# Sorted attention and a gated feed-forward on one core: five value blocks sorted from the loaded tile, and the first stage's calls listed anew

## The chip, the core and the metric

The kernel runs on one core of a Trainium2 chip. The core has TensorE for matrix products (with a separate row for its weight loads), VectorE, ScalarE and GpSimd (POOL) for the rest, and SyncE, which here issues transfers only. All engines take their instructions in order. The metric is the device time of one execution in microseconds; the kernel before takes 231.41 us, the median of three runs (231.49, 230.86, 231.41).

## The reference

```
for _ in range(5):                                   # P: sort_net, 8 x 8 per head
    P = exp(P - max(P, -1)); P = P / (sum(P, -1) + 1e-9); P = P / (sum(P, -2) + 1e-9)
k_sorted = einsum('bhij,bhjcd->bhicd', P, k_blocks)  # 8 blocks of 96 keys
v_sorted = einsum('bhij,bhjcd->bhicd', P, v_blocks)
scores = (q_block @ k_sorted_block.T) / 8            # each block attends to its own block
attn   = softmax(scores);  x = attn @ v_sorted_block
h = x @ w_in;  out = (h * cos(h)) @ w_out
```

There are 4 batches of 8 heads, 768 positions and 64 columns, so x is 3072 x 512; w_in is 512 x 2048 and w_out 2048 x 512. Output is 3072 x 512 in float32.

## The kernel before

The 3072 rows are cut into eight **chunks** n of 384 rows: batch n // 2, and the first or second four blocks of 96 positions. A chunk has four units u, one block of positions each, for all eight heads. Per unit: scores (`s_ps`, later `qs`, `bt`), their maximum and difference on VectorE (`s_max`, `s_sub`, or `qk_reduce`), the exponential on ScalarE (`expo`), its transpose (by TensorE as `p_ps` and `p_ev`, or by a DMA transpose from SyncE's queue), the product with the sorted values (`av_products`), its normalisation on VectorE (`av_norm`) and a second transpose (`x_ps`, `x_ev`, or `xp`, `xe`). With the chunk's rows transposed, the feed-forward runs "up" (`up_four`, `uh`: products with w_in; `cos_four`, `uc`: the cosine on ScalarE; `gate_four`, `ug`: the product on VectorE) and "down" (`down_four`, `dn`: products with w_out; `down_out`, `dc`: the copy out and its store).

Ahead of that, the 8 x 8 matrices are normalised (`rounds`, lines 346 to 394) and spread into block matrices (`bds`, `bdv`), and keys and values are sorted by products with them: `kp` and `k_place` make the first batch's keys in three tiles t, of which half 0 serves chunk 0 and half 1 chunk 1 (`kxp` copies half 1 across partitions on POOL); `ks` and `kse` those of the second batch; `v0` and `v0e` the first batch's values in eight blocks z of eight columns. The products of a block z read their weights either straight from the loaded tile (`vv`, one column every 64 elements) or from `vperm`, a copy with the columns gathered that POOL makes (`v_permute`). The constant VN (line 202) says how many of the 64 columns are read directly: below it `v0` takes `vv` and writes two results per instruction (line 798), from it on `vperm`. VN also sets how much of the second batch's half of the value tile POOL clears (line 388), how much of `vperm` ScalarE zeroes (line 366) and how much `z_vperm` clears later (line 754).

The order is written out by hand (`manual_schedule`, line 63): lines 1028 to 1561 list the calls, and each engine and each DMA queue runs its own share of them in that order. Waits between engines come from the data and from tiles that are used again: three double tiles (`big`, tag B), two single ones (`acc`, tag C), three score tiles and so on. Loads, with a cast from float32, are issued by POOL and so stand in POOL's order; DMA transposes and stores are issued by SyncE. `p_hold` and `hold` (line 613) are one-element copies on POOL that wait for a DMA transpose, so that the loads listed after them are not issued earlier. `load_pair` loads both batches of the second pair, keys into `pair`, values into `vbuf`. `keep_warm` products (`fill=`) fill waits with products of zeros.

The change touches VN; lines 1028 to 1215, which hold chunk 0 and the attention of chunk 1; the value loads at lines 1237 to 1239 and 1317; the hold at 1316; `dn(1, 1, 2)` and `dn(1, 1, 3)` at 1307 and 1311; the evictions `xe(2, 1)` and `xe(2, 0)` at 1335 and 1339; and the eviction `be("vs", 2)` at 1409.

Of the kernel before, what the change touches and what calls it, by code (L numbers as in the profile page):

```python
# [18 lines left out]
def kernel(  # L19
# [157 lines left out]
    def v_permute(rows, lo=0, halves=True, step=VQ, hi=D):  # L177

        for z in range(lo, hi, step):
            dst = vperm[rows, :CD].rearrange("p (d c) -> p d c", d=D)[:, z:z + step]
            src = vv[rows, z:z + step, :blk]
            if halves:
                dst = dst.rearrange("p d (x t) -> p d x t", x=2)
                src = src.rearrange("p d (t x) -> p d x t", x=2)
            nc.gpsimd.tensor_copy(dst, src)  # L187
# [14 lines left out]
    VN = 32  # L202
# [833 lines left out]
    kp(0, *B)  # L1036
    k_place(0, A, 0)
    k_place(0, V, 1)
    v_permute(slice(0, 64), 56, False, 8, 64)
    kp(1, *B)  # L1040
    k_place(1, A, 0)
    k_place(1, A, 1)
    v0(0, *C)
    v0e(0, A)
    s_ps(0, 0)
    s_max(0, 0)
    s_sub(0, 0)
    s_ps(0, 1)
    v0(3, *C)
    v0(2, *B)  # L1050
    v0e(3, A)
    v0e(2, A)
    s_max(0, 1)
    s_sub(0, 1)
    expo(0, 0, True)
    v0(1, *C)
    v0e(1, A)
    v0(5, *C)
    s_ps(0, 3)
    s_ps(0, 2)  # L1060
    s_max(0, 3)
    s_max(0, 2)
    v0e(5, A)
    expo(0, 1, True)
    s_sub(0, 3)
    load_w_out(0)
    v0(4, *C)
    v0e(4, A)
    v0(6, *C, fill=1)
    v0(7, *B)  # L1070
    v0e(7, A)
    p_ps(0, 1, *C, fill=2)
    p_ev(0, 1, V)
    v0e(6, A)
    expo(0, 3, True)
    p_ps(0, 0, *B, fill=2)
    p_ev(0, 0, A)
    av_products(0, 1, fill=2)
    s_sub(0, 2)
    av_norm(0, 1, True)  # L1080
    load_w_out(1)
    av_products(0, 0)
    p_ps(0, 3, *B)
    av_norm(0, 0, True)
    load_w_out(2)
    load_w_out(3)
    kxp(2)
    kxp(0)
    expo(0, 2, True)
    p_ps(0, 2, *C)  # L1090
    x_ps(0, 1, *B)
    p_ev(0, 2, V)
    x_ps(0, 0, *C)
    kxp(1)
    p_ev(0, 3, A)
    x_ev(0, 1, A)
    av_products(0, 3)
    x_ev(0, 0, V)
    av_products(0, 2)
    up_four(0, 2, 0)  # L1100
    up_four(0, 2, 1)
    cos_four(0, 2)
    av_norm(0, 3, True)
    x_ps(0, 3, *B)
    q_products(1, 0, 0, 16, *C)
    av_norm(0, 2, True)
    z_turned(1)
    load(kbuf, 0, kin_d[1])
    x_ev(0, 3, V)
    load(vbuf, 64, vin_d[1])  # L1110
    q_products(1, 1, 0, 16, *C)
    x_ps(0, 2, *B)
    x_ev(0, 2, A)
    up_four(0, 0, 0)
    gate_four(0, 2)
    up_four(0, 0, 1)
    cos_four(0, 0)
    picks(pick_pair, (2, 3))
    up_four(0, 1, 0)
    up_four(0, 1, 1)  # L1120
    cos_four(0, 1)
    gate_four(0, 0)
    up_four(0, 3, 0)
    up_four(0, 3, 1)
    up_four(1, 0, 0)
    gate_four(0, 1)
    cos_four(0, 3)
    gate_four(0, 3)
    z_vperm()
    up_four(1, 0, 1)  # L1130
    q_place_half(1, 0, 1, A)
    q_place_half(1, 0, 0, V)
    cos_four(1, 0)
    gate_four(1, 0)
    up_four(1, 2, 0)
    up_four(1, 2, 1)
    q_place_half(1, 1, 0, A)
    z_turned(0)
    q_place_half(1, 1, 1, V)
    up_four(1, 3, 0)  # L1140
    up_four(1, 3, 1)
    up_four(1, 1, 0)
    p_pads()
    down_four(1, 0)
    cos_four(1, 2)
    gate_four(1, 2)
    load_q(2)
    last = block([pick_pair[:]], *C)
    cos_four(1, 3)
    gate_four(1, 3)  # L1150
    spread(bds[1], last)
    s_ps(1, 0)
    s_max(1, 0)
    s_ps(1, 1)
    up_four(1, 1, 1)
    cos_four(1, 1)
    s_max(1, 1)
    s_sub(1, 0)
    expo(1, 0, True)
    down_four(0, 0)  # L1160
    down_four(0, 1)
    down_four(0, 2)
    ks(5, *B)
    gate_four(1, 1)
    s_sub(1, 1)
    kse(5, A)
    s_ps(1, 3)
    down_four(0, 3)
    expo(1, 1, True)
    load_pair(pair, kin_d, 0 * CD // 2, 1 * CD // 2)  # L1170
    s_max(1, 3)
    s_sub(1, 3)
    p_ps(1, 0, *B)
    s_ps(1, 2)
    s_max(1, 2)
    s_sub(1, 2)
    load_pair(pair, kin_d, 1 * CD // 2, 2 * CD // 2)
# [3 lines left out]
    down_four(1, 1)  # L1181
    p_ps(1, 1, *B)
    v_permute(slice(64, 128), 48, True, 16, 64)
    down_out(0, A)
    p_ev(1, 0, A)
    expo(1, 3, True)
    av_products(1, 0)
    av_norm(1, 0, True)
    ks(4, *C)
    down_four(1, 2)  # L1190
    p_ev(1, 1, A)
    av_products(1, 1)
    p_ps(1, 3, *B)
    p_ev(1, 3, V)
    kse(4, A)
    av_norm(1, 1, True)
    expo(1, 2, True)
    down_four(2, 0)
    p_ps(1, 2, *B)
    p_ev(1, 2, A)  # L1200
    av_products(1, 3)
    av_norm(1, 3, True)
    down_four(1, 3)
    av_products(1, 2)
    down_out(1, A)
    x_ps(1, 1, *B)
# [3 lines left out]
    x_ps(1, 0, *B)  # L1210
    x_ps(1, 3, *B)
    av_norm(1, 2, True)
# [94 lines left out]
    dn(1, 1, 2)  # L1307
# [3 lines left out]
    dn(1, 1, 3)  # L1311
    dc(1, 1, nc.sync)
# [3 lines left out]
    p_hold(2, 2)  # L1316
# [18 lines left out]
    xe(2, 1, None, V)  # L1335
# [3 lines left out]
    xe(2, 0, None, V)  # L1339
# [67 lines left out]
    bt(('vs', 1, A), ('vs', 2, A))  # L1407
    be("vs", 1, A)
    be("vs", 2, A)
# [181 lines left out]
```

## Time and profile before

| | |
|---|---|
| median of three runs | 231.41 us |
| profiled execution, its own time | 230.85 us |
| its span | 229.1 us |
| granted TensorE clock | 1.00 |
| TensorE busy | 219.3 us, 96% |
| weight loads busy | 137.4 us, 60% |
| VectorE, ScalarE busy | 171.8 us (75%), 153.0 us (67%) |
| POOL busy | 95.2 us, 42% |
| moved by DMA | 31.21 MB |

The span runs from the first to the last instruction that the profiler recorded; the profiled execution's own time is 1.75 us longer. All times inside the kernel are counted from the span's start. A row of the timeline has the start, the duration of the group, the engine, the line, the operation, the tiles and shapes and, in brackets, how long the engine idled before and what ended the wait. Durations of successive matmuls overlap, since they are pipelined. A row of transfers ends with the time from issue to landing.

### The profile page before, as it was taken

The numbers are of one execution on the slowest core, as the hardware profiler recorded it, in microseconds if no ns is written. First come the engines' busy times: TensorE is split into PE (matmuls) and PEld (weight loads), VectorE is DVE, ScalarE is ACT, GpSimd is POOL, SyncE is SP. The second block draws the span as 40 slices with busy tenths as digits, with TensorE's granted clock in tenths as the row PEclk, the third lists the DMA queues.
The fourth block names the chain that finished last, engine by engine and source line by source line (L and its number), as shares of the span: only waits on it lengthen the run. The fifth ranks groups of instructions, "written<-read, shape, count | busy, mean of one in ns | idle before, by whom it ended". The sixth has DMA issues, their size and how long they took to land.

```text
span 229.1 us, 5513 instructions
## 1 busy us (share of the span) xinstructions
PE 219.3 (96%) x2243; PEld 137.4 (60%) x2265; DVE 171.8 (75%) x297; ACT 153.0 (67%) x206; POOL 95.2 (42%) x120
## 2 busy tenths in 40 slices
PE   8688899999999999999999999999999999999994
PEld 3387798567665566645665456655655566555554
DVE  6779859987798768868589967987699769646700
ACT  5749865966989758897688466736674667716521
POOL 7999999299960288934517001800000000000000
PEclk9999999999999999999999999999999999999999
DMA  5999999996999699857979639953934440351012
GB/s 65 237 187 207 204 205 234 198 230 172 99 120 206 172 157 132 146 126 152 165 146 129 118 70 164 201 92 73 189 119 85 89 158 0 69 147 46 0 46 94
DMA packets 67833, 31.21 MB, mean 136 GB/s; under 512 B 56416, under 2 KB 63200, under 8 KB 67552
## 3 DMA queue, kind: packets, MB, share of 16 engines
q0 software_dynamic: 24048, 13.64, 43.4%
q1 hardware_dynamic: 43472, 17.02, 33.8%
q8 instruction: 18, 0.29, 0.6%
q10 hardware_dynamic: 288, 0.20, 0.3%
q14 instruction: 7, 0.06, 0.1%
HBM read 27.27 MB, written 6.29 MB: 147 GB/s over the span
## 4 chain that ended last, share of the span: by engine, by line
PE 80%; DVE 12%; ACT 4%; issue 2%; DMA 1%; ACTq 0%; DVEq 0%
PE h L687 18%; PE o L712 16%; PE h L915 14%; PE o L1012 11%; PE av L643 3%; DVE mx L839 3%; DVE s L843 3%; PE sc L457 3%; PE h L876 2%; PE ks L424 2%; PE o L897 2%; DVE gg L888 2%; PE o L1555 2%; ACT p_buf L587 1%; PE xps L966 1%
## 5 line engine op out<-in xcount | busy, mean ns | idle before, releaser
L687 PE MATMUL h<-xT,w_in_t 128*128 128x384 bf16 x256 | 43.2, 327 | 0.0
L691 ACT ACTIVATE c<-h,half_pi 128x768 f32<-128x768 f32 x32 | 28.8, 900 | 17.7 <-PE h L687 17.7
L712 PE MATMUL o<-w_out_t,gg 128*128 128x512 bf16 x169 | 39.9, 379 | 0.4
L695 DVE TENSOR_TENSOR gg<-c,h 128x768 bf16<-128x768 f32 x32 | 29.9, 950 | 11.6 <-ACT c L691 11.6
L915 PE MATMUL h<-xT,w_in_t 128*128 128x384 bf16 x192 | 35.2, 327 | 0.1
L687 PEld LDWEIGHTS <-w_in_t 128*128 128x128 bf16 x256 | 24.7, 98 | 16.2
L1012 PE MATMUL o<-w_out_t,gg 128*128 128x512 bf16 x134 | 33.7, 379 | 0.6 <-issue 0.3
L187 POOL COPY vperm<-kv 64x768 bf16<-64x768 bf16 (+2 forms) x12 | 28.4, 2417 | 4.8 <-DMA kv<-in_v_dram 4.8
L587 ACT ACTIVATE p_buf<-s 96x768 bf16<-96x768 f32 x32 | 26.6, 843 | 4.5 <-DVE s L509 4.0
L927 DVE TENSOR_TENSOR gg<-c,h 128x768 bf16<-128x768 f32 x24 | 22.7, 948 | 7.6 <-ACT c L921 7.6
L921 ACT ACTIVATE c<-h,half_pi 128x768 f32<-128x768 f32 x24 | 21.6, 900 | 8.3 <-PE h L915 7.4
L712 PEld LDWEIGHTS <-gg 128*128 128x128 bf16 x176 | 16.0, 98 | 16.5
L509 DVE TENSOR_TENSOR s<-sc,mx 96x384 f32<-96x384 f32 (+1 forms) x33 | 24.3, 735 | 1.6
L507 DVE TENSOR_REDUCE mx<-sc 96x4 f32<-96x384 f32 (+1 forms) x33 | 24.0, 728 | 0.4 <-PE sc L522 0.4
L915 PEld LDWEIGHTS <-w_in_t 128*128 128x128 bf16 x192 | 17.5, 98 | 9.9 <-DVE xT L267 0.3
L656 DVE TENSOR_TENSOR xn<-av,r 96x512 bf16<-96x512 f32 x32 | 22.0, 686 | 1.1
L1012 PEld LDWEIGHTS <-gg 128*128 128x128 bf16 x144 | 12.6, 97 | 12.0
L138 POOL DMA_DIRECT2D kv<-in_q_dram x24 | 16.0, 676 | 0.8 <-issue 0.8
L265 ACT COPY kv<-o 128x512 f32<-128x512 f32 (+2 forms) x10 | 5.2, 523 | 14.0 <-PE o L712 8.5
L265 ACT CAST kTs<-ks 128x512 bf16<-128x512 f32 (+1 forms) x17 | 10.4, 633 | 4.6 <-PE ks L424 4.6
L654 DVE RECIPROCAL r<-av 96x8 f32<-96x8 f32 x32 | 6.3, 197 | 7.3 <-PE av L643 7.1
L267 DVE COPY kv<-o 128x512 f32<-128x512 f32 (+1 forms) x5 | 3.1, 611 | 11.3 <-PE o L1555 8.5
(140 smaller groups left out, 335.9 us busy)
## 6 DMA issues: line engine op xcount, KB each, us to landing
out_dram<-kv SPq DMA_DIRECT2D x12, 256.0 KB, 2.7
out_dram<-o_s SPq DMA_DIRECT2D x10, 256.0 KB, 2.6
w_in_t<-in_moe_w_in_dram POOLq DMA_DIRECT2D x4, 512.0 KB, 12.0
w_out_t<-in_moe_w_out_dram POOLq DMA_DIRECT2D x4, 512.0 KB, 12.5
kv<-in_k_dram POOLq DMA_DIRECT2D x2, 768.0 KB, 10.3
kv<-in_v_dram POOLq DMA_DIRECT2D x2, 768.0 KB, 13.5
pair<-in_k_dram POOLq DMA_DIRECT2D x2, 768.0 KB, 13.2
kv<-in_v_dram POOLq DMA_DIRECT2D x6, 256.0 KB, 5.5
```

What stands on the lines that cost most here:

```text
L187: nc.gpsimd.tensor_copy(dst, src)
L507: nc.vector.reduce_max(mx[:], scv, axis=AX.X)
L509: nc.vector.tensor_tensor(s, scv, mx.to_broadcast(list(s.shape)), op=ALU.subtract)
L587: nc.scalar.activation(p[:, :, :blk], s_t.pop((n, u)).rearrange("p e h c -> p (e h) c"), AF.Exp, scale=scale)
L656: nc.vector.tensor_tensor(xn.rearrange("p h e d -> p e h d"), avv[:, :, :, :D], r.to_broadcast([blk, 2, H2, D]), op=ALU.mult)
L687: nc.tensor.matmul(h[:, f2, :w], w_in_t[:, kk, f * 128:(f + 1) * 128], xT[n][:, kk], start=(kk == 0), stop=(kk == KC - 1))
L691: nc.scalar.activation(c[:], h[:, :, :w], AF.Sin, bias=half_pi[:, 0:1])
L695: nc.vector.tensor_tensor(gt[n, fp // 2][:, f:f + 2], c[:], h[:, :, :w], op=ALU.mult)
L712: nc.tensor.matmul(o[:], gt[n, f // 4][:, f % 4, ts * 128:(ts + 1) * 128], w_out_t[:, f, :], start=(f == 0), stop=(f == FC - 1))
L915: nc.tensor.matmul(h[:, f2, :TC], w_in_t[:, kk, f * 128:(f + 1) * 128], xT[n][:, kk], start=(kk == 0), stop=(kk == KC - 1))
L927: nc.vector.tensor_tensor(gt[n, fp // 2][:, f:f + 2], ps.pop(("c", n, fp))[:], ps.pop(("h", n, fp))[:, :, :TC], op=ALU.mult)
L1012: nc.tensor.matmul(out_ps[n, ts][:], gt[n, q][:, f % 4, ts * 128:(ts + 1) * 128], w_out_t[:, f, :], start=(f == 0), stop=(f == FC - 1))
```

## The change

VN becomes 40, so that block 4 of the values is read from the loaded tile as well, and POOL copies three blocks instead of four. The list of chunk 0 and of chunk 1's attention is written in a new order. The maxima of units 1 and 0 come before the differences; the first units of "up" are 0, 3, 2, 1 instead of 2, 0, 1, 3; `down_four(0, 0)` comes between "up" products; chunk 1's scores begin with unit 3. Several key, weight and x copies change between VectorE and ScalarE, and the `fill` products stand elsewhere. The values' load of the second batch stands later in the list, though its place among POOL's own calls is the same.

In chunk 1 the first three of six value loads of the next pair move from before `uh(1, 0)` to the other three, and the hold in front of them waits for the transpose of unit 1, not unit 2. `dn(1, 1, 2)` comes after the products of unit (2, 0), `dn(1, 1, 3)` after the scores (3, 0). Two evictions of xT go from VectorE to ScalarE, one of sorted values from ScalarE to VectorE.

```diff
-    VN = 32
+    VN = 40
...
     kp(2, *B)
-    v_permute(slice(0, 64), 32, False, 8, 40)
-    v_permute(slice(0, 64), 40, False, 8, 48)
+    kp(1, *B)
+    k_place(1, A, 0)
+    kp(0, *B)
+    v0(0, *C)
     k_place(2, V, 1)
     k_place(2, V, 0)
+    v_permute(slice(0, 64), 40, False, 8, 48)
+    k_place(1, V, 1)
     v_permute(slice(0, 64), 48, False, 8, 56)
...
+    s_ps(0, 1)
+    s_max(0, 1)
+    k_place(0, A, 1)
+    v0e(0, A)
     v_permute(slice(0, 64), 56, False, 8, 64)
...
+    v0(5, *B)
+    v0e(5, A)
+    v0(2, *C)
+    v0(3, *C)
+    v0e(2, A)
     s_max(0, 0)
+    s_sub(0, 1)
+    v0e(3, A)
     s_sub(0, 0)
...
+    up_four(0, 0, 0)
+    up_four(0, 0, 1)
+    cos_four(0, 0)
+    av_norm(0, 2, True)
+    gate_four(0, 0)
+    q_products(1, 0, 0, 16, *C)
+    q_place_half(1, 0, 1, V)
...
+    x_ev(0, 3, V)
+    up_four(0, 1, 0)
     cos_four(0, 2)
...
+    s_ps(1, 3)
+    s_max(1, 3)
+    s_sub(1, 3)
     up_four(0, 1, 1)
     cos_four(0, 1)
...
+    gate_four(0, 1)
+    down_four(0, 0)
     up_four(1, 0, 0)
...
     hold_keys()
-    load_pair(vbuf, vin_d, 0 * CD // 6, 1 * CD // 6)
-    load_pair(vbuf, vin_d, 1 * CD // 6, 2 * CD // 6)
-    load_pair(vbuf, vin_d, 2 * CD // 6, 3 * CD // 6)
     uh(1, 0)
...
-    dn(1, 1, 2)
     expo(2, 3, True)
     av_products(2, 0)
     av_norm(2, 0, True)
-    dn(1, 1, 3)
-    dc(1, 1, nc.sync)
+    dn(1, 1, 2)
     bt(('sc', 3, 0), ('ks', 1, A))
     qr2(3, 0)
     be("ks", 1, A)
-    p_hold(2, 2)
+    dn(1, 1, 3)
+    dc(1, 1, nc.sync)
+    p_hold(2, 1)
+    load_pair(vbuf, vin_d, 0 * CD // 6, 1 * CD // 6)
+    load_pair(vbuf, vin_d, 1 * CD // 6, 2 * CD // 6)
+    load_pair(vbuf, vin_d, 2 * CD // 6, 3 * CD // 6)
     load_pair(vbuf, vin_d, 3 * CD // 6, 4 * CD // 6)
...
-    xe(2, 1, None, V)
+    xe(2, 1, None, A)
...
-    xe(2, 0, None, V)
+    xe(2, 0, None, A)
...
-    bt(('vs', 1, A), ('vs', 2, A))
+    bt(('vs', 1, A), ('vs', 2, V))
     be("vs", 1, A)
-    be("vs", 2, A)
+    be("vs", 2, V)
```

More of the change, by code (lines that the diff above doesn't have):

```diff
@@ L1100 @@
+    load(kbuf, 0, kin_d[1])
+    x_ps(0, 2, *B)
+    x_ev(0, 2, V)
+    q_place_half(1, 0, 0, V)
+    up_four(0, 3, 0)
+    up_four(0, 3, 1)
+    q_place_half(1, 1, 1, V)
     up_four(0, 2, 0)
     up_four(0, 2, 1)
-    cos_four(0, 2)
[L1103 to L1113, printed above, removed]
@@ L1138 @@
+    load(vbuf, 64, vin_d[1])
+    gate_four(1, 2)
+    picks(pick_pair, (2, 3))
+    last = block([pick_pair[:]], *C)
+    spread(bds[1], last)
+    s_max(1, 0)
+    z_vperm()
+    s_sub(1, 0)
     z_turned(0)
[L1139 to L1142, printed above, removed]
+    down_four(0, 2)
+    ks(4, *C)
+    kse(4, A)
     p_pads()
+    ks(5, *B)
+    down_four(0, 3)
+    load_q(2)
     down_four(1, 0)
-    cos_four(1, 2)
-    gate_four(1, 2)
-    load_q(2)
@@ L1148 @@
[L1148 to L1156, printed above, removed]
+    load_pair(pair, kin_d, 0 * CD // 2, 1 * CD // 2)
+    p_ps(1, 3, *B)
+    kse(5, A)
+    s_ps(1, 2)
     s_max(1, 1)
-    s_sub(1, 0)
+    s_sub(1, 1)
+    down_four(1, 1)
+    load_pair(pair, kin_d, 1 * CD // 2, 2 * CD // 2)
     expo(1, 0, True)
-    down_four(0, 0)
-    down_four(0, 1)
-    down_four(0, 2)
@@ L1163 @@
[L1163 to L1172, printed above, removed]
     p_ps(1, 0, *B)
[L1174 to L1177, printed above, removed]
+    p_ev(1, 3, A)
     v_permute(slice(64, 128), 0, True, 16, 16)
@@ L1209 @@
     down_four(2, 2)
-    x_ps(1, 0, *B)
-    x_ps(1, 3, *B)
-    av_norm(1, 2, True)
     down_four(2, 3)
```

141 lines of the change are left out of this document (65 added, 76 removed).

## The prediction

> **What bounds the kernel now.** I read the page first, then busy time by stage, then the chain of waits, then each engine in order of time around the edits.
>
> ```profile
> span 229.1 us, 5513 instructions
> PE 219.3 (96%) x2243; PEld 137.4 (60%) x2265; DVE 171.8 (75%) x297; ACT 153.0 (67%) x206; POOL 95.2 (42%) x120
> PE 80%; DVE 12%; ACT 4%; issue 2%; DMA 1%; ACTq 0%; DVEq 0%
> ```
>
> TensorE is busy 96% of the span and holds 80% of the chain; VectorE holds 12%. Where those 12% lie, the stages tell (after the bounds: their length, then busy us of PE, PEld, DVE, ACT, POOL):
>
> ```profile
> 14.00:20.00 6.00, 5.73 (x135) 5.33 (x132) 5.79 (x8) 5.01 (x10) 5.81 (x4) 1.00 1.24 207
> 20.00:25.00 5.00, 3.98 (x73) 3.32 (x73) 4.93 (x9) 4.78 (x8) 4.78 (x10) 1.00 1.30 203
> 25.00:30.00 5.00, 5.00 (x98) 4.65 (x96) 3.93 (x9) 3.45 (x5) 4.84 (x9) 1.00 1.27 206
> 30.00:35.00 5.00, 5.00 (x64) 5.00 (x62) 3.10 (x4) 3.88 (x5) 4.89 (x5) 1.00 1.24 207
> 35.00:40.00 5.00, 4.84 (x66) 4.01 (x65) 4.61 (x8) 2.77 (x4) 4.87 (x10) 1.00 1.13 230
> 40.00:45.00 5.00, 4.95 (x51) 2.96 (x50) 4.97 (x7) 4.82 (x7) 0.60 (x2) 1.00 1.10 197
> 45.00:50.00 5.00, 4.77 (x70) 3.18 (x69) 4.64 (x10) 3.87 (x6) 5.00 (x2) 1.00 1.09 230
> ```
>
> From 14 to 25 us VectorE is full (10.72 of 11) and TensorE has room: chunk 0's four score tiles are reduced there. From 25 us on TensorE is full; it idles 0.44 us in 25 to 50. So a call listed anew after 25 us can win tenths at most, and what is won before 25 us is won once. The granted clock is 1.00 in every row.
>
> **Step 1: value block 4 from the loaded tile.** POOL loses one of four copies; TensorE reads eight more weights with a stride.
>
> ```profile
> 16.00 2.34 PE L800 MATMUL vs<-bdv,kv 128*128 128x128 bf16 x24
> 20.21 0.66 PE L800 MATMUL vs<-bdv,vperm 128*128 128x64 bf16 x16
> ```
> ```profile
> 10.65 1.37 POOL L388 MEMSET kv<- 64x1536 f32 x1
> 12.93 0.82 POOL L128 DMA_DIRECT2D q_mem<-in_q_dram  x1
> 14.19 5.87 POOL L187 COPY vperm<-kv 64x768 bf16<-64x768 bf16 x4 [0.44 <-DMA kv<-in_v_dram]
> ```
>
> A direct block takes 2.34/3 = 0.78 us, a copied one 0.66/2 = 0.33: +0.45 us on TensorE. It lies before 25 us, where TensorE idles 6.00 − 5.73 + 5.00 − 3.98 = 1.29 us waiting for VectorE and ScalarE; without that cover it costs 0.45. POOL's chain of copies ends at 14.19 + 3 × 1.47 = 18.6 instead of 20.06 us. In exchange the zeros behind the values grow from 32 to 40 columns: 1.37 × 40/32 = 1.71, +0.34 us, ahead of POOL's loads and copies. The copies waited 0.44 us for the values to land, so this is covered with 0.1 us left. The later clearing of the copied tile (z_vperm) grows by a quarter too, less than the 1.47 us POOL saved; ScalarE's zero copies shrink. Step 1: 0.
>
> **Step 2: the order up to the first "up" product.** Both maxima now precede both subtractions.
>
> ```profile
> 15.76 0.96 DVE L839 TENSOR_REDUCE mx<-sc 96x8 f32<-96x768 f32 x1
> 16.75 0.99 DVE L843 TENSOR_TENSOR s<-sc,mx 96x768 f32<-96x768 f32 x1
> 19.50 1.81 DVE L839 TENSOR_REDUCE mx<-sc 96x8 f32<-96x768 f32 x2
> 21.23 0.94 DVE L843 TENSOR_TENSOR s<-sc,mx 96x768 f32<-96x768 f32 x1
> 24.26 0.19 DVE L654 RECIPROCAL r<-av 96x8 f32<-96x8 f32 x1
> ```
> ```profile
> 22.21 0.84 ACT p_buf L587
> 26.16 1.44 PE h L876 x16
> ```
>
> A subtraction that needs the maximum just before it starts 0.99 us after it (15.76, 16.75); independent ones follow in 0.87 (two maxima from 19.50, next at 21.23: 1.73/2). Two such pairs are parted: 2 × 0.12 = 0.24 us. The start does not move: the first scores need the same key halves, two copies on each engine, as before. The third subtraction thus starts at 15.76 + 6 × 0.87 = 20.98 instead of 21.23. ScalarE gives back part: the same eight value copies and two exponentials precede the third exponential, which starts at about 22.2 as before, and its product's reciprocal (24.26) hardly moves. What follows on VectorE still gains a little. I take −0.15; bounds 0 (ScalarE sets it) and −0.35 (ScalarE follows, and the last waits before 26.16 close as well).
>
> **Step 3: 26 to 55 us listed anew.** The same products, cosines, gates, scores and copies; only their places move. TensorE's idle above (0.44, some of it inherent) bounds the gain. New waits are possible. The batch's next queries:
>
> ```profile
> q_mem<-in_q_dram POOLq DMA_DIRECT2D x1, 384.0 KB, 14.4
> ```
>
> They land at 12.93 + 14.4 = 27.3 us; the transposes that use them come right after the first 16 matmuls, at about 26.0 + 1.44 = 27.4: hardly any slack. If the 0.34 us of step 1 delays the landing too, that much is added. The scores of (1,3) now want a tile that the gate of (0,3) frees, and that gate stands on VectorE behind another gate and four copies; either engine can be there last. The values' load keeps its place among POOL's own calls; the pair loads, now held by the later "block", are issued some 2 us later but queue behind loads still under way. I take 0; ends −0.3 and +0.6.
>
> **Step 4: the value loads behind p_hold.** Three loads leave 63 to 65 us and join three others, and the hold in front now waits for weights (2,1), not (2,2).
>
> ```profile
> 63.46 1.64 POOL L101 DMA_DIRECT2D kv<-in_v_dram  x3
> 78.50 0.18 POOL L615 CAST held<-p_turned 96x1 f32<-96x1 bf16 x1 [11.55 <-DMA p_turned<-p_buf]
> ```
> ```profile
> q_turned<-kv SPq DMA_TRANSPOSE x1, 7.3
> ```
> ```profile
> p_turned<-p_buf SPq DMA_TRANSPOSE x1, 4.0
> ```
> ```profile
> p_turned<-p_buf SPq DMA_TRANSPOSE x1, 2.9
> ```
> ```profile
> kv<-p_buf SPq DMA_TRANSPOSE x1, 7.7
> ```
> ```profile
> 71.92 4.78 SPq L607 DMA_TRANSPOSE p_turned<-p_buf  x3
> ```
> ```profile
> 76.01 0.42 PE L643 MATMUL av<-vS,p_turned 96*128 96x65 bf16 x8
> 80.06 0.41 PE L643 MATMUL av<-vS,p_turned 96*128 96x65 bf16 x8
> 80.52 0.34 PE L966 MATMUL xps<-order,xn 96*128 96x96 bf16 x4
> 82.20 0.73 PE L966 MATMUL xps<-order,xn 96*128 96x96 bf16 x8
> ...
> 109.20 0.51 PE L966 MATMUL xps<-ident,xn 96*128 96x96 bf16 x8
> ```
>
> The four landing times are those of the query transpose issued right behind the three loads (7.3 us), of weights (2,0), issued at 71.92 behind that transpose (4.0: landed at 75.9, just before the product at 76.01), of weights (2,2), alone (2.9), and of weights (3,0), issued among the later loads (7.7). With the loads gone I expect 2.9 for (2,0): landed at 74.8. The list uses this: the product comes one quarter of "down" (0.86 us) earlier, as do the scores (3,0), and two evictions go to ScalarE, so the normalisations come earlier and three gaps close: before 76.01 (about 0.15), before 80.52 (80.06 + 0.24 for eight products = 80.30: 0.22) and in the eight transposes from 82.20 (0.73 against 0.51 for the unbroken eight at 109.20: 0.2). Together 0.57; −0.4 taken, 0 and −0.57 the ends. POOL's copies behind the six loads start later by what three more loads take, less the earlier hold (2.1 us, below); their readers stand among chunk 2's "down" products, behind all its "up" products, which is the cover.
>
> **Step 5: one copy of sorted values to VectorE.**
>
> ```profile
> 102.17 1.93 ACT L265 CAST pair<-vs 96x1024 bf16<-96x1024 f32 x2
> ```
> ```profile
> 102.25 0.20 DVE L654 RECIPROCAL r<-av 96x8 f32<-96x8 f32 x1 [1.72 <-PE av L643]
> ```
> ```profile
> 102.05 1.03 PE L1012 MATMUL o<-w_out_t,gg 128*128 128x512 bf16 x4
> 103.24 0.40 PE L643 MATMUL av<-vS,p_turned 96*128 96x65 bf16 x8 [0.15 <-ACT pair L265]
> ```
>
> The product at 103.24 waits for the first of two copies on ScalarE; four matmuls after 102.05 are done at 102.91. VectorE idles 1.72 us before 102.25. No row shows such a copy there; ScalarE takes 1.93/2 = 0.97 us for it, and VectorE 0.94 to 0.99 to read 768 columns of such a tile in the rows of step 2, so 1024 take up to 0.99 × 4/3 = 1.32. Begun within VectorE's idle time, it ends by about 102.5, and its tile is free before 102.91. Worth 0.3; bounds 0 and 0.33.
>
> **The sum** against the profiled execution's own 230.85 us (span 229.1): −0 − 0.15 + 0 − 0.4 − 0.3 = −0.85, so 230.0; its median lies 0.56 higher at 231.41, so 230.56, forecast 230.6.
>
> **The rivals.** *A, eaten in step 3* (chance 0.17): TensorE stalls 0.5 us on tiles or queries and step 4 gives half: −0.15 + 0.5 − 0.2 − 0.3 = −0.15, 231.3. For it: the waits above have no slack. Against: VectorE still idles in 25 to 35. *B, the loads meet weights (2,2)* (0.15), the slower side: the three issues take 1.6 us each by their row, so (2,1) starts at 73.5 and (2,2) at 75.1; the hold frees POOL at 73.5 + 2.9 = 76.4, not 78.5, and six loads follow while (2,2) is under way. Under loads the row shows 7.7 us in place of 2.9: landed at 82.8, wanted at 80.06 − 0.4 = 79.7, a stall of 3.1: 231.41 − 0.85 + 3.1 = 233.7; a half-slowed one (5.3) stalls 0.7: 231.3. It decides once the transpose takes more than 4.6 us, and is slower than before from 5.5. Against it: (2,2) has 1.3 us ahead of the loads' issue. [...] *C, weights (2,0) are no faster* (0.08): landed at 75.9 while TensorE is there at 74.9; 1.0 lost, step 4 becomes +0.6: 231.41 − 0.15 + 0.6 − 0.3 = 231.6. *D, all gains at their ends* (0.08): −0.35 − 0.3 − 0.57 − 0.33 = −1.55: 229.9. The forecast keeps 0.52.
>
> **How the numbers follow.** 0.3% is 0.69 us, about what a measurement here tells from none (the three runs spread over 0.63). The forecast's own spread (230.1 to 231.0) is faster in four fifths: 0.42, with D 0.50. Same: the rest of the forecast 0.10, A 0.17, most of C 0.06: 0.33. Slower: B 0.15, C 0.02: 0.17. The range leaves out the far end of B and a little beyond D: 229.6 to 232.0.
>
> **What would show it.** Step 1: three copies on POOL ending near 18.6, five direct value blocks of 0.78 us. Step 2: subtractions 0.87 us apart, first "up" product near 26.0. Step 3: chunk 1's first product 0 to 0.4 us earlier. Step 4: query transpose near 4 us, first (2,·) product at 74.8 without a wait, (2,2) not waited for. Step 5: no wait for a pair copy near 102.5. Wrong it is if TensorE idles over 0.6 us in 25 to 50, or waits for weights near 80 us.

## The result and the profile after

The changed kernel takes 234.01 us (median of four, 233.39 to 237.16) beside 231.13 us for the kernel before on the same chip (four, 230.84 to 231.49): a ratio of 1.0115, 95% interval 1.0074 to 1.0156. It is slower, and the time lies outside the forecast range of 229.6 to 232.0. The ratios here leave out executions more than 1.5% above the fastest of their kernel, which ran at lower granted clocks: 237.16 us (clock 0.991; the other three 0.998), and further down 236.47 us in e2 (0.985) and 286.73 us in e11 (0.758). The profiled execution's own time is 234.52 us, 3.67 more than the 230.85 us of the profile before.

The page of the kernel after: its span, busy time by engine, and the shares of the chain that ended last.

```profile
span 232.8 us, 5531 instructions
PE 221.8 (95%) x2263; PEld 137.5 (59%) x2263; DVE 173.2 (74%) x298; ACT 152.0 (65%) x205; POOL 94.8 (41%) x119
...
PE 79%; DVE 8%; ACT 6%; DMA 4%; issue 2%; ACTq 0%; DVEq 0%
```

VectorE's share of the chain fell from 12% to 8%, as the new list meant, but ScalarE's rose from 4% to 6% and transfers' from 1% to 4%. Four percent of 232.8 us is 9 us that the chain spent in transfers. Where time was lost, the first "up" product of each stage tells. The rows of TensorE's timeline, before:

```profile
26.11 1.07 PE L876 MATMUL h<-xT,w_in_t 128*128 128x192 bf16 x11
...
55.66 1.47 PE L915 MATMUL h<-xT,w_in_t 128*128 128x384 bf16 x8
...
83.63 1.46 PE L915 MATMUL h<-xT,w_in_t 128*128 128x384 bf16 x8
...
110.41 1.46 PE L915 MATMUL h<-xT,w_in_t 128*128 128x384 bf16 x8
```

and after, with TensorE's waits between them:

```profile
18.67 0.19 PE L800 MATMUL vs<-bdv,kv 128*128 128x64 bf16 x1 [0.86 <-issue]
...
26.63 0.57 PE L876 MATMUL h<-xT,w_in_t 128*128 128x192 bf16 x5
...
33.09 0.50 PE L457 MATMUL sc<-kTs,q_turned 128*128 128x96 bf16 x8 [0.40 <-DVE gg L888]
...
56.58 0.66 PE L915 MATMUL h<-xT,w_in_t 128*128 128x384 bf16 x3
...
78.83 0.42 PE L643 MATMUL av<-vS,p_turned 96*128 96x65 bf16 x8 [0.17 <-DMA p_turned<-p_buf]
...
84.46 0.81 PE L915 MATMUL h<-xT,w_in_t 128*128 128x384 bf16 x4
...
106.58 0.42 PE L643 MATMUL av<-vS,p_turned 96*128 96x65 bf16 x8 [2.67 <-DMA p_turned<-p_buf]
...
113.77 0.98 PE L915 MATMUL h<-xT,w_in_t 128*128 128x384 bf16 x5
```

| stretch | before, us | after, us | difference |
|---|---|---|---|
| to the first "up" product of chunk 0 | 26.11 | 26.63 | +0.52 |
| to that of chunk 1 | 29.55 | 29.95 | +0.40 |
| to that of chunk 2 | 27.97 | 27.88 | −0.09 |
| to that of chunk 3 | 26.78 | 29.31 | +2.53 |
| to the end (229.08 and 232.75) | 118.67 | 118.98 | +0.31 |

So most of the loss lies in one stretch, around one wait: 2.67 us at 106.58 for the turned weights of unit (3,1), the next chunk's. The same place by windows (length, then busy us of PE, PEld, DVE, ACT, POOL, with the granted clock, the share of DMA and GB/s behind), before and after:

```profile
100.00:105.00 5.00, 4.69 (x71) 2.67 (x71) 2.52 (x6) 4.10 (x6) 0.00 (x0) 1.00 0.75 158
105.00:110.00 5.00, 4.84 (x73) 2.77 (x73) 3.65 (x6) 4.34 (x5) 3.55 (x7) 1.00 0.68 124
```
```profile
100.00:105.00 5.00, 3.92 (x54) 1.88 (x52) 3.39 (x5) 4.02 (x6) 5.00 (x2) 1.00 1.11 163
105.00:110.00 5.00, 3.42 (x66) 2.08 (x67) 2.49 (x5) 0.99 (x2) 1.08 (x4) 1.00 0.92 187
```

TensorE works 7.34 us of these ten where it worked 9.53. What is late ahead of it stands in POOL's timeline, before and after (the loads, the last part of the queries of chunk 4, the copies of values):

```profile
78.95 1.60 POOL L101 DMA_DIRECT2D kv<-in_v_dram  x3 [0.27 <-issue]
...
86.58 0.67 POOL L138 DMA_DIRECT2D q_mem<-in_q_dram  x1 [0.74 <-DMA kv<-in_v_dram]
87.25 11.26 POOL L187 COPY vperm<-kv 128x1536 bf16<-128x1536 bf16 x4
```
```profile
78.94 0.18 POOL L615 CAST held<-p_turned 96x1 f32<-96x1 bf16 x1 [13.39 <-DMA p_turned<-p_buf]
79.41 3.23 POOL L101 DMA_DIRECT2D kv<-in_v_dram  x6 [0.29 <-issue]
...
93.26 0.67 POOL L138 DMA_DIRECT2D q_mem<-in_q_dram  x1 [1.58 <-DMA kv<-in_v_dram]
93.93 8.49 POOL L187 COPY vperm<-kv 128x1536 bf16<-128x1536 bf16 x3
```

and in the timeline of SyncE's queue, before and after (transposes of those queries, swap of the keys' halves, transposes of the weights (3,·)):

```profile
91.70 3.60 SPq L158 DMA_TRANSPOSE q_turned<-q_mem  x2
...
96.53 0.59 SPq L438 DMA_DIRECT2D kTs<-kTs  x1
99.44 2.80 SPq L607 DMA_TRANSPOSE p_turned<-p_buf  x2
```
```profile
96.62 3.62 SPq L158 DMA_TRANSPOSE q_turned<-q_mem  x2
...
101.48 1.24 SPq L438 DMA_DIRECT2D kTs<-kTs  x1
102.82 2.89 SPq L607 DMA_TRANSPOSE p_turned<-p_buf  x2
```

The query transposes start 4.92 us later (96.62 for 91.70): the three added loads stand ahead of the queries on POOL, and while it issued the queries' eight parts POOL waited 5.9 us, in six waits, for value loads to land (before: 1.3 us, in two). On SyncE's queue the weights (3,1), listed behind those transposes and the key swap, are issued at 102.82, behind the swap's row (101.48 + 1.24 = 102.72), and not at 99.44. The chain of waits of the kernel after holds that transfer itself (start, us, what), behind that of the weights (2,1):

```profile
74.15 4.64 DMA p_turned<-p_buf
...
102.82 3.72 DMA p_turned<-p_buf
```

102.82 + 3.72 = 106.54, and the product follows at 106.58.

### The profile page after: what moved, and what is told of

Read it like the earlier page. It is cut to its first block, busy times and chain, and to the rows that moved or that the text cites. A ratio compares the mean times of both kernels' runs of the same rounds, so it can differ in the third digit from the quotient of the medians.

```text
span 232.8 us, 5531 instructions
## 1 busy us (share of the span) xinstructions
PE 221.8 (95%) x2263; PEld 137.5 (59%) x2263; DVE 173.2 (74%) x298; ACT 152.0 (65%) x205; POOL 94.8 (41%) x119
## 4 chain that ended last, share of the span: by engine, by line
PE 79%; DVE 8%; ACT 6%; DMA 4%; issue 2%; ACTq 0%; DVEq 0%
PE h L687 18%; PE o L712 16%; PE h L915 13%; PE o L1012 9%; PE h L876 4%; DMA p_turned<-p_buf 4%; PE av L643 3%; PE sc L457 3%; PE o L897 2%; ACT p_buf L587 2%; PE ks L424 2%; PE o L1554 2%; DVE s L843 1%; PE vs L800 1%; DVE mx L839 1%
## 5 line engine op out<-in xcount | busy, mean ns | idle before, releaser
L712 PE MATMUL o<-w_out_t,gg 128*128 128x512 bf16 x176 | 41.1, 379 | 0.0
L1012 PE MATMUL o<-w_out_t,gg 128*128 128x512 bf16 x144 | 34.9, 379 | 0.0
L187 POOL COPY vperm<-kv 64x1536 bf16<-64x1536 bf16 (+2 forms) x11 | 27.0, 2498 | 2.0 <-DMA kv<-in_v_dram 2.0
L712 PEld LDWEIGHTS <-gg 128*128 128x128 bf16 x176 | 16.1, 98 | 16.5
L138 POOL DMA_DIRECT2D q_mem<-in_q_dram x16 | 10.8, 680 | 6.2 <-DMA kv<-in_v_dram 5.9
```

What stands on the lines that cost most here:

```text
L138: nc.gpsimd.dma_start(out=q_heads[:, i, :, e], in_=src[:, ih * IC + i, :, e])
L712: nc.tensor.matmul(o[:], gt[n, f // 4][:, f % 4, ts * 128:(ts + 1) * 128], w_out_t[:, f, :], start=(f == 0), stop=(f == FC - 1))
L1012: nc.tensor.matmul(out_ps[n, ts][:], gt[n, q][:, f % 4, ts * 128:(ts + 1) * 128], w_out_t[:, f, :], start=(f == 0), stop=(f == FC - 1))
```

## The experiments

All ratios are against the kernel before on the same chip (its medians were 230.93 to 231.18 us).

| run | median, us | ratio | 95% interval |
|---|---|---|---|
| e1_loads_back | 231.97 | 1.0045 | 1.0019 to 1.0071 |
| e2_loads_only | 235.07 | 1.0188 | 1.0141 to 1.0234 |
| e3_queries_first | 235.47 | 1.0202 | 1.0154 to 1.0250 |
| e7_weights_first | 239.96 | 1.0370 | 1.0335 to 1.0405 |
| e5_fill | 232.92 | 1.0068 | 1.0053 to 1.0084 |
| e10_gate_apart | 232.70 | 1.0059 | 1.0045 to 1.0073 |
| e11_order_back | 231.44 | 1.0008 | 0.9998 to 1.0019 |
| e4_zeros_only | 231.40 | 1.0007 | 0.9994 to 1.0021 |
| e13_block1_early | 231.71 | 1.0026 | 1.0017 to 1.0035 |
| e8_copy_only | 231.21 | 1.0001 | 0.9991 to 1.0011 |
| e6_chunk1_list | 232.04 | 1.0044 | 1.0029 to 1.0059 |
| e14_block1_free_tile | 232.26 | 1.0068 | 1.0045 to 1.0091 |
| e15_one_warm_less | 231.32 | 1.0019 | 1.0009 to 1.0030 |
| e16_no_fill | 231.31 | 1.0019 | 1.0003 to 1.0036 |
| e17_head_only | 231.96 | 1.0044 | 1.0030 to 1.0058 |
| e18_before_one_warm_less | 231.14 | 1.0004 | 0.9993 to 1.0015 |
| e19_down_first | 231.80 | 1.0031 | 1.0019 to 1.0044 |

### Is it the loads? e1, e2

e1 is the changed kernel with the loads and the hold as they were; e2 is the kernel before with them as changed.

```diff
 # e1, against the changed kernel
-    p_hold(2, 1)
-    load_pair(vbuf, vin_d, 0 * CD // 6, 1 * CD // 6)   # and two more
+    p_hold(2, 2)
...
     hold_keys()
+    load_pair(vbuf, vin_d, 0 * CD // 6, 1 * CD // 6)   # and two more
```

> The changed kernel with the three value loads back in front of chunk 1's first up product and the hold back on weights (2,2). Theory Q (queue): the six loads stand ahead of the queries of chunk 4 and make them land at 96.7 instead of 91.8 us; SyncE's queue waits for them, so that weights (3,1) are issued at 102.8 instead of 99.4 and TensorE waits 2.7 us for them. Then here that wait goes, less up to 0.6 us that the early loads cost the transposes near 75 us: 231.2 to 231.9, with the product of (3,1) near 104. Theory L (list): the new order of chunk 0, which is 0.9 us behind at chunk 1's first up product, is what costs; then at most 0.5 us goes: 233.5 or more.

> The kernel before with only the three value loads moved to the other three and the hold on weights (2,1). Theory Q: the wait for weights (3,1) appears here too, 2.5 to 3 us less up to 0.4 won near 75 us: 233.3 to 234.0. Theory L: within 0.5 us of before, 230.7 to 231.6.

Putting the loads back takes the wait for the weights (3,1) away: the stretch to chunk 3 is 26.78 us in e1, as before. Moving the loads alone makes the kernel before slower by 1.9%, with the same wait (TensorE's timeline of e2):

```profile
105.10 0.41 PE L643 MATMUL av<-vS,p_turned 96*128 96x65 bf16 x8 [2.23 <-DMA p_turned<-p_buf]
```

So the moved loads carry the main loss. The profiled execution of e2 is its fastest, 232.76 us, which the 2.23 accounts for. The other three (235.06, 236.47, 235.09) had mean granted clocks of 0.993, 0.985 and 0.993 where it had 0.999: 0.006 of 233 us is 1.4 of the 2.3 us between the fastest and the next, an estimate. Where in them the clock fell is not recorded.

### Which queue? e3, e7

e3 puts the queries of chunk 4 ahead of the six loads on POOL; e7 leaves POOL alone and puts the query transposes and the key swap behind the weights on SyncE.

```diff
 # e3, against the changed kernel
     p_hold(2, 1)
+    load_q(4)
     load_pair(vbuf, vin_d, 0 * CD // 6, 1 * CD // 6)   # and five more
-    load_q(4)
...
 # e7, against the changed kernel
-    q_transpose_dma(4)
...
-    k_swap_b(0)
...
     expo(3, 1)
     expo(3, 2)
+    q_transpose_dma(4)
+    k_swap_b(0)
```

> The changed kernel with the queries' load of chunk 4 issued ahead of the six value loads. Theory Q: the queries land near 86, SyncE's queue is free when the weights (3,1) are ready, and the wait of 2.7 us goes: 231.0 to 231.6. Theory T (traffic): six loads in a row slow every transpose behind them, whatever their order (weights (3,1) took 3.7 instead of 2.9 us): 233.0 to 234.5, with a wait left at the product of (3,1).

> The changed kernel with the transposes of chunk 4's queries and the key swap listed behind the weights (3,1) and (3,2) on SyncE's queue; the loads stay late. Theory Q: the weights are issued at 100.2 when they are ready, land near 103.1, and the wait of 2.7 us goes, though the queries land as late as in the changed kernel: 231.0 to 231.8. Theory T: the weights still land late, 233 or more.

Neither gives the time back; both move the wait. In e3 (SyncE's queue, then TensorE) the transposes run under the loads, and the copies that follow the loads come late:

```profile
86.38 12.28 SPq L158 DMA_TRANSPOSE q_turned<-q_mem  x2
```
```profile
101.32 0.61 PE L535 MATMUL vs<-bd,vperm 64*128 64x64 bf16 x16 [2.27 <-DVE s L509]
```

The products' row names VectorE, that of their weight loads POOL's copies of `vperm`. These began at 87.25 before and at 93.93 in the changed kernel; here they begin at 98.47, two in 5.57 us, so the first is done at about 101.26. VectorE's subtraction ends then too (100.32 + 0.95), but in the changed kernel, with the same lists for both engines, these products start at 98.99, ahead of that subtraction (100.42). So it is the copies:

```profile
101.32 0.45 PEld L535 LDWEIGHTS <-vperm 64*128 64x128 bf16 x16 [2.42 <-POOL vperm L187]
...
98.47 5.57 POOL L187 COPY vperm<-kv 128x1536 bf16<-128x1536 bf16 x2 [10.61 <-DMA kv<-in_v_dram]
```

In e7 the weights (3,1) leave SyncE at 100.17 and the product that waited 2.67 us no longer waits for them. Now the scores of chunk 4 wait for the swapped keys:

```profile
111.00 0.20 PE L522 MATMUL sc<-kTs,q_turned 64*128 64x96 bf16 x1 [4.55 <-DMA kTs<-kTs]
```

The expectation that reordering would bring back 231 failed twice. Part of both times is the granted clock, which fell behind these waits (0.993 and 0.984 over the spans; last section). From 79 us on, loads, queries, key swap and weights had no slack for three more loads in any of the three orders run, and what stood last in the queue was waited for: 2.67 us for the weights (3,1), 2.27 for the copies in e3, 4.55 for the swapped keys in e7.

### The prediction's small steps alone: e4, e8, e6

```diff
 # e4, against the kernel before (step 1)
-    VN = 32
+    VN = 40
...
-    v_permute(slice(0, 64), 32, False, 8, 40)
 # e8, against the kernel before (step 5); e6 has this and chunk 1's new list,
 # with the loads as before
-    bt(('vs', 1, A), ('vs', 2, A))
+    bt(('vs', 1, A), ('vs', 2, V))
     be("vs", 1, A)
-    be("vs", 2, A)
+    be("vs", 2, V)
```

> The kernel before with the five direct value blocks alone (one copy fewer on POOL, 40 columns of zeros in place of 32). The prediction's step 1: 0, so 231.1 (230.9 to 231.4), with POOL's copies ending near 18.6 and the first up product at 26.1. Rival: the 0.45 us of slower strided products are not covered in the order of the kernel before, and the time is 231.5 to 231.6 with the first up product at 26.5.

> The kernel before with step 5 alone: the second copy of sorted values of chunk 3 on VectorE. The prediction's step 5: minus 0.3, so the product at 103.24 starts 0.3 earlier and the stage from the first product of uh(2) to that of uh(3) is 26.5 us in place of 26.78; 230.8. Rival, from e1_loads_back: VectorE's copy takes 1.22 us where ScalarE's takes 0.97, the product waits for the other copy, which stays on ScalarE, and the stage stays at 26.8: 231.1.

> The kernel before with the edits of chunks 1 to 3 other than the value loads: the products (2,0) a quarter of down earlier, two evictions on ScalarE, the copy of step 5 on VectorE; the three early loads stay early. Theory (weights bound): the weights (2,0) land at about 75.9 whatever the list says, the product waits some 0.9 us for them at 75.0, and nothing is won behind it: the stretch 55.7 to 84 is 28.0 to 28.8 us in place of 27.97 and the time is 231.1 to 232.0. Rival (the prediction's step 4 without its loads): the gaps close and the time is 230.6 to 230.9.

e4 is level, with its first "up" product at 26.07: step 1 costs nothing, as predicted. e8 is level too. Its ScalarE and TensorE rows:

```profile
102.12 1.01 ACT L265 CAST pair<-vs 96x1024 bf16<-96x1024 f32 x1
```
```profile
103.18 0.40 PE L643 MATMUL av<-vS,p_turned 96*128 96x65 bf16 x8
```

The copy that stayed on ScalarE still starts at 102.12 and ends at 103.13; the product still follows it. e6 is 0.9 us slower: the weights (2,0), wanted earlier, are waited for.

```profile
75.87 0.42 PE L643 MATMUL av<-vS,p_turned 96*128 96x65 bf16 x8 [0.74 <-DMA p_turned<-p_buf]
```

The list wants the weights (2,0) early, and they land as late as before (3.9 us after their issue; 4.0 before).

### What remains of the first half: e5, e10, e11

These build on e1. e5 adds a product of zeros ahead of the scores (0,3), e10 also moves half of an "up" ahead of the scores (1,3), e11 also puts chunk 1's "down" calls back in their old order.

```diff
 # e5, against e1
-    s_ps(0, 3)
+    s_ps(0, 3, fill=1)
 # e10, against e5
+    up_four(0, 1, 1)
     s_ps(1, 3)
     s_max(1, 3)
     s_sub(1, 3)
-    up_four(0, 1, 1)
 # e11, against e10
+    dn(1, 1, 2)
     expo(2, 3, True)
     av_products(2, 0)
     av_norm(2, 0, True)
-    dn(1, 1, 2)
+    dn(1, 1, 3)                      # and dc(1, 1, nc.sync)
     bt(('sc', 3, 0), ('ks', 1, A))
     qr2(3, 0)
     be("ks", 1, A)
-    dn(1, 1, 3)                      # and dc(1, 1, nc.sync)
```

> The kernel is e1_loads_back with one product that nobody reads (a warm-up product) put between value block 3 and the scores (0,3). Theory H (held product): in the changed kernel the last product of value block 3 is held behind the next weight load, which waits for VectorE's subtraction; ScalarE's copy of block 3 therefore starts at 18.9 and everything on ScalarE up to the first up product comes late. With the extra product in between, block 3 is done near 18.0, ScalarE's copy starts near 18.0, the first up product at about 26.0 in place of 26.3 (e1_loads_back), and the time is 0.3 to 0.4 below e1_loads_back's 231.97: about 231.6. Rival V (VectorE sets the first up product whatever ScalarE does): the copy of block 3 starts earlier, but the first up product stays at 26.3 or later, and the time stays at 232.0.

> The kernel is e5_fill with the second half of up(0,1) listed ahead of the scores (1,3), so that the tile which the gate of (0,3) frees is wanted 0.7 us later. Theory: the wait of 0.40 us for that gate (at 33.1 in the changed kernel) goes and nothing takes its place; the stretch from the first up product to the first of chunk 1 is 29.6 us, as before the change (29.55) and not 29.95, and the time is 0.4 below e5_fill: about 231.2. Rival: VectorE is full there, the gate of (0,1) and later waits come late by the same amount, and the stretch stays at 29.9; the time is that of e5_fill.

> The kernel is e10_gate_apart with chunk 1's down calls in the order of the kernel before (a quarter of down ahead of the products (2,0) again), so that with the early value loads the weights (2,0) are not wanted before they land. Theory: av(2,0) waited up to 2.0 us for weights in e1_loads_back and does not here; the time is 0.3 to 0.8 below e10_gate_apart's, 230.5 to 230.9, and within 0.3% of the kernel before or just under it. Rival: the wait for weights (2,0) in e1_loads_back was of one execution, and the order makes no difference (within 0.2 us of e10_gate_apart).

e5 missed: block 3 is still held (0.92 us), the first "up" product is at 26.68, and its profiled execution waits 1.01 us for the weights (2,0). That wait varies: 2.03 us in e1's profiled execution (233.75; e1's median is 231.97), 0.82 in e4's, 1.28 in e16's, none in those of before, e11 and e15.

The early loads alone do not decide how late these weights land. In e2, without the early loads, they took 3.8 us; in e15, with them, 2.8. In all 19 traces the landing goes with the packets on the queue for instructions, of which one falls between 72.8 and 76.6 us. Of the three transposes of weights (2,0), (2,1) and (2,2), those under way with such a packet took 3.5 to 5.2 us, and the others 2.8 to 3.0; only in e3 and e7 does a packet that starts in the last 0.3 us of one leave it at 2.8. The packet starts at 73.2 in the kernel before and at 72.8 in e2, within (2,0); at 75.5 in e15 and 76.2 in the changed kernel, behind it, and there (2,1) took 4.5 and 4.6. This is seen and not tested: no run was made to move that packet.

e10 takes the 0.40 us wait for the gate away, but the stretch shrinks only from 29.95 to 29.76: 0.20 us comes back as a wait of the next "up" products for a subtraction on VectorE. e11 gains 1.26 us over e10, since nothing waits for the weights (2,0) in its profile; it is level with the kernel before. So chunk 1's new list, in the places where that packet fell, costs about 1 us with the early loads (e6 says 0.9).

### The held product: e13 to e18

In every kernel with the new list so far the first "up" product came late (26.29 to 27.01 us), and value block 3's last product ran at 18.4 to 18.7, after TensorE had stood idle for 0.5 to 0.9 us. The first theory was that the next weight load, which waits for VectorE, holds it. e13 and e14 put value block 1 between, in two tiles.

```diff
 # e13, against e11 (e14: *C for *B)
-    s_ps(0, 3, fill=1)
+    v0(1, *B)
+    s_ps(0, 3)
...
-    v0(1, *B)
```

> The kernel is e11_order_back without the warm-up product of e5_fill (which itself wrote the blocked score tile and so was held too) and with value block 1 listed ahead of the scores (0,3): its eight products need neither the blocked tile nor anything late. Theory H (a product is held behind the next one on TensorE that waits): now the last product of block 1 is the one held, block 3 is done near 17.8, ScalarE's copy of it starts near 17.9 in place of 18.6, the exponential behind it at about 18.5, the first up product at 25.7 to 26.0 in place of 26.38, and the time is 0.4 to 0.6 below e11_order_back: 230.8 to 231.0. Rival V (VectorE's four reductions set the first up product): it stays at 26.3 to 26.4 and the time at 231.4.

> The kernel is e13_block1_early with value block 1 in another tile: in e13 block 1 took the very tile that VectorE's subtraction of (0,1) frees (its weight load waited 0.85 us for it) and the scores (0,3) moved to the tile freed by the subtraction after it, so that run could not tell H from V. Here block 1 takes the tile of value block 2, which ScalarE has copied out at 17.8. Theory H (the last product of block 3 is held because the next weight load on TensorE waits): it is no longer held until 18.4 to 18.7 but done by about 18.0, ScalarE's copy of block 3 starts at 17.9 to 18.0 in place of 18.64 to 18.96, the third maximum on VectorE follows the second subtraction at 19.25, the first up product comes at 25.7 to 26.0 in place of 26.38 (e11_order_back) and the time is 0.4 to 0.6 below e11_order_back's 231.44, about 230.9. Rival I (the hold belongs to that place in the instruction stream, whatever stands behind it): the product is held to 18.4 or later once more, and the first up product stays at 26.3 or later. Rival V (VectorE sets the first up product): the copy comes early, the first up product stays at 26.3.

In e13 block 1 landed in the blocked tile and says nothing. In e14 its tile was free at 17.79 (ScalarE's copy, from 16.48, took 1.31 for two), and TensorE still stopped until 18.56, waiting for nothing that the profile shows:

```profile
18.56 0.94 PE L800 MATMUL vs<-bdv,kv 128*128 128x64 bf16 x9 [0.75 <-issue]
```

The theory fell. What the kernels share is the count. Windows from 0 to 18.2 us of before, after and e14 (products and weight loads in brackets):

```profile
0.00:18.20 18.20, 14.78 (x221) 9.75 (x222) 13.48 (x58) 11.00 (x22) 16.12 (x25) 1.00 0.93 165
```
```profile
0.00:18.20 18.20, 15.39 (x221) 9.43 (x222) 13.54 (x58) 10.74 (x21) 16.24 (x25) 1.00 0.94 164
```
```profile
0.00:18.20 18.20, 14.33 (x220) 9.25 (x222) 13.51 (x58) 10.74 (x21) 16.33 (x25) 1.00 0.94 164
```

Each has run 222 weight loads and stops (a product's record is missing here and there), the kernel before as well, whose list is another (there the next block also needs POOL's copies, so that it alone would show nothing). The transfers of the kernel after from 16 to 17 us hold one packet on the queue for instructions:

```profile
q8 instruction: 1, 0.02, 6.1%
```

6.1% of 16 engines for 1 us is 0.98 us for a packet of 16 KB. The queue has 18 such packets in the kernel after (0.29 MB on its page), spread along TensorE's work: 396 of its products and weight loads had begun at the first and 4489 at the last, 241 from one to the next in the mean (144 to 300). If TensorE stops at the end of the code that it has, then one product fewer at the very start moves the stop by one product. e15 does that to e11; e16 also drops e5's product of zeros; e18 does it to the kernel before; e17 is the kernel before with the new list up to the first "up" product alone, and one product fewer.

```diff
 # e15 (against e11), e16, e17, e18
-    keep_warm(14, big.tile([128, 512], FP32, name="idle", tag="big"))
+    keep_warm(13, big.tile([128, 512], FP32, name="idle", tag="big"))
```

> The kernel is e11_order_back with 13 warm-up products at the start in place of 14: one weight load and one product fewer ahead of everything. In every trace so far, the kernel before among them, TensorE stops once it has run 222 weight loads and 221 or 222 products, and goes on 2.2 to 2.4 us after the packet of 16 KB on the queue named instruction that starts at 16.1 to 16.4, whatever stands there. Theory I (the next piece of TensorE's code is not there): the stop moves one product down the list, behind value block 3, whose last product is then done by 17.8; ScalarE's copy of block 3 starts at 17.9 to 18.0 in place of 18.64, TensorE still goes on at 18.4 to 18.7, the first up product comes at 25.8 to 26.1 in place of 26.38, and the time is 0.2 to 0.6 below e11_order_back: 230.9 to 231.2. Rival H (the product is held because the next weight load waits for VectorE until 18.45): the last product of block 3 is held to 18.4 as before, the first up product stays at 26.3 or later. Rival V: the copy comes early, the first up product stays.

> The kernel is e15_one_warm_less without the warm-up product of e5_fill in front of the scores (0,3): the version in which everything that cost time in the changed kernel is undone (loads, chunk 1's order, the gate's wait, the held product). Theory I: ScalarE's copy of block 3 at 17.9 to 18.0 too, the scores (0,3) 0.3 us earlier than in e15, the first up product at 25.7 to 26.0, and the time is 230.7 to 231.1, level with the kernel before (231.1) or up to 0.2% under it. Rival H or V: the first up product at 26.3 or later, 231.4.

> The kernel before with the change's list up to the first up product alone (with its five direct value blocks) and 13 warm-up products in place of 14, so that TensorE's stop for code does not hold value block 3; everything from the first up product on is the kernel before, the three early value loads among it. Theory I: the prediction's step 2 is right as far as the order goes, and the stop alone spoiled it: the first up product at 25.8 (before 26.11), every later mark 0.2 to 0.3 earlier, and the time 0.2 to 0.3 below the kernel before: a ratio of 0.9985 to 0.999. What can take it back: the weights (2,0) land at 75.9 and are then wanted at 75.7, so up to 0.3 may be waited for there; then the ratio is 0.999 to 1.000. Rival: the new list costs time for another reason, and the first up product is at 26.1 or later with a ratio of 1.000 or more.

> The kernel before with 13 warm-up products at the start in place of 14, and nothing else: the control for e15 to e17. Theory I: TensorE's stop moves one product down the list; in the kernel before it came at 18.1 behind value block 1, where the next block waits for POOL's and VectorE's work until 18.37 anyway, so nothing is won: the first up product at 26.1, ratio 1.000. Rival (one warm-up product fewer is itself worth time): the first up product at 25.8, ratio 0.9985.

In e15 the same window shows 221 weight loads, and block 3 is done: the next load, of the product of zeros, waits for VectorE's subtraction until 18.48. ScalarE's three value copies run without a break; they end at 18.46 (e11: 19.23):

```profile
0.00:18.20 18.20, 13.68 (x220) 9.01 (x221) 13.54 (x58) 11.06 (x22) 16.58 (x25) 1.00 0.95 167
```
```profile
16.44 2.02 ACT L265 CAST vS<-vs 96x512 bf16<-96x512 f32 x3 [0.22 <-PE vs L800]
```

The first "up" product comes at 26.09 (e11: 26.38), and without the product of zeros at 25.82 (e16, TensorE's timeline):

```profile
25.82 1.40 PE L876 MATMUL h<-xT,w_in_t 128*128 128x192 bf16 x15
```

The times did not follow, though 0.2 to 0.6 below e11 was expected: both ratios are 1.0019, e11's is 1.0008. e16's profiled execution loses its gain to the 1.28 us for the weights (2,0); in e15's, 0.20 us is left at TensorE's last group of products (222.49 for 222.69), and the span is 0.1 longer all the same.

e18 stays at 26.08 with a ratio of 1.0004: the missing product is itself worth nothing. But the stop moved there too: again 222 weight loads have run, the last of them now for the block that began at 18.37 before. Its product runs, and the other seven wait for nothing that the profile shows:

```profile
18.15 0.19 PE L800 MATMUL vs<-bdv,vperm 128*128 128x64 bf16 x1
18.51 0.39 PE L800 MATMUL vs<-bdv,vperm 128*128 128x64 bf16 x7 [0.17 <-issue]
```

So the place of TensorE's stop in the list is shown; that it is the arrival of code fits the packets and the count, but no row names it.

e17 has its first "up" product at 25.82 as well and reaches chunk 1 at 55.37, 0.29 earlier than before, and loses it all to one wait:

```profile
76.89 0.42 PE L643 MATMUL av<-vS,p_turned 96*128 96x65 bf16 x8 [1.17 <-DMA p_turned<-p_buf]
```

The weights (2,0), issued at 72.02, took 4.8 us in e17 where they took 4.0 (its packet starts at 74.6, within them). e19 gives them 0.86 us more:

```diff
 # e19, against e17
     expo(2, 3, True)
+    dn(1, 1, 3)
     av_products(2, 0)
     av_norm(2, 0, True)
-    dn(1, 1, 3)
```

> The kernel is e17_head_only with one more quarter of down (0.86 us of TensorE) listed ahead of the products (2,0), which in e17 waited 1.17 us at 76.9 for the weights (2,0). Theory: e17's head gives 0.29 at the first up product and loses it to that wait alone; with the quarter of down in front the wait shrinks to 0.3 or nothing, the stretch from 55.4 to the next chunk's first product is 28.0 to 28.3 us in place of 29.13, and the time is 230.8 to 231.2, a ratio of 0.9985 to 1.000. Rival: VectorE's normalisation of (2,0), now 0.9 later, delays the transposes and the next chunk, and the time stays at 231.7 to 232.

The wait shrinks to 0.38, but 0.60 us for VectorE's normalisation, now late, follows it, and the stretch is 29.02 us: the rival was right. No version here beats the kernel before.

## Why the prediction was wrong

**Step 4 failed, and with it the forecast** (−0.4; the stretches to chunks 2 and 3 came to −0.09 and +2.53). It followed the three loads on POOL to the copies behind them, found cover there, and stopped. The queries of chunk 4 stand between the loads and those copies. They were not followed: to their landing, the transposes that need them, and SyncE's queue, where the key swap and the weights (3,1) stand behind. That path, put at nothing, made the wait of 2.67 us. The cover named for the copies did hold (TensorE did not wait for them). The weights (2,0) took 2.8 us where 2.9 was expected, and their product at 75.91 did not wait. That was luck: the step gave the loads as the reason, but e2 has 3.8 us without the early loads and e15 2.8 with them. For the weights (2,1) it took an issue at 73.5 and 2.9 us; they were issued at 74.15 and took 4.64. So their product waited 0.17 us at 78.83, the hold ended at 78.94, and the loads began 0.46 later than before, not 2.1 earlier.

**Rival B** (233.7, weights (2,2) under loads) came near the time and was not the reason: the product (2,2) at 81.16 waited for nothing. Its thought, that more late loads hurt a transpose, was right one step further down SyncE's queue (2.67 us of waiting for the weights (3,1)).

**Step 1**, 0: right (e4, 1.0007). **Step 2**, −0.15 with bounds 0 and −0.35: VectorE did as worked out (the third subtraction at 20.97 for 20.98), yet the first "up" product came 0.52 later, outside the bounds. The step took ScalarE's start for unchanged; TensorE now reached its stop at 17.81 (18.67 − 0.86; before, the 24 products ended at 18.34), with block 3 not quite done, and ScalarE waited for it. With the stop one product further the order gains 0.29 (e16, e17), within the bounds. The 0.52 is of one execution: e1, with the same list up to there, has 26.29 (+0.18). In e1 the packet for instructions starts near 16.15 and the stop ends at 18.35; in the kernel after it is 16.35 and 18.67.

**Step 3**, 0 with bounds −0.3 and +0.6: +0.40, by the wait that the step named (the gate of (0,3) before the scores (1,3)). The other named risk, the queries at 27.3, did not come true. One of the prediction's signs of being wrong showed, just: TensorE idled 0.66 us in 25 to 50, the sign being over 0.6.

**Step 5**, −0.3: 0 (e8, 1.0001). The step read that the product waits for the first of two copies and then moved the second. The first keeps its place on ScalarE.

The last +0.31 us lie behind TensorE's work: its last group of products, before and after, starts 111.80 us after chunk 3's first "up" product (222.21 − 110.41, 225.57 − 113.77).

```profile
222.21 3.70 PE L1555 MATMUL o<-w_out_t,gg 128*128 128x256 bf16 x48
```
```profile
225.57 3.70 PE L1554 MATMUL o<-w_out_t,gg 128*128 128x256 bf16 x48
```

The granted clock of 0.998 took no part: it is below 1.00 only from 231 us on, behind the last product. Why the end took 0.31 us longer is open.

## What to carry to other kernels

When a transfer is moved in a queue, follow every call behind it on that queue to its landing, and then every queue that waits for that landing, until a row shows slack. Moving the sufferer only passed the wait on where the whole stretch was full (2.27 us in e3, 4.55 in e7). A wait that the profile puts down to "issue" at the same count of instructions in every version (here 222 weight loads) can belong to the count and not to what stands next; its place in the list can be tried by a product more or less ahead of it (e15, e18). A landing time is put down to a neighbour only after a run without that neighbour (e2) and a look at all traces.

## What the runs showed of the hardware

In the kernels with 14 warm-up products and the new list, TensorE stopped after 222 weight loads, whatever stood next, and went on at 18.4 to 18.7 us, 2.1 to 2.5 us after a 16 KB packet for instructions (0.29 MB in 18) that starts between 16.1 and 16.4. It stood idle for 0.5 to 0.9 us, with a DMA share of 1.24 in 14 to 20 us before and after; that it waited for code was not shown. A DMA transpose beside such a packet took 3.5 to 5.2 us, the same without one 2.8 to 3.0 (the weights (2,·) of 19 traces).

The granted clock fell after some single waits and not after others. The page's row of the clock, in 40 slices, of e3 (a wait of 2.27 us at 99.05) and of e7 (4.55 us at 106.45):

```profile
PEclk9999999999999999979999999999999999999999
```
```profile
PEclk9999999999999999998599999999999999999999
```

The mean clock is 0.993 in e3 and 0.984 in e7, and 0.999 in e2 with a wait of 2.23. By windows of 1 us, e3's is 0.67, 0.50, 0.50 and 0.63 from 101 to 105, and 1.00 on either side: 1.7 us lost, an estimate. The second of them (the first number behind the brackets is the clock):

```profile
102.00:103.00 1.00, 1.00 (x3) 0.30 (x2) 0.00 (x0) 0.99 (x1) 1.00 (x1) 0.50 1.03 179
```

The length of the wait does not tell these cases apart: behind the 2.67 us from 103.91 in the changed kernel, more than e3's 2.27, the windows up to 110 have 1.00, and so has e2's from 84 to 110. What else sets them apart was not shown.
